# Linear attention and two MLPs on one core: the first two tiles' attention product in fp32, and w_in joined in place

## The chip, the cores and the metric

One core of a Trainium2 chip runs the whole program. The metric is the time of one execution in device microseconds. Before the change it is 1578.94 us, the median of three runs (1578.28 to 1579.91).

## The reference

```python
q_s = softmax(q, over the 64 of a head);  k_s = softmax(k, over the 576 of the sequence)
kv = einsum('bhsd,bhse->bhde', k_s, v)
x = einsum('bhsd,bhde->bhse', q_s, kv)      # 8 batches, 8 heads, 576 x 64; 1e-9 in each denominator
x = x.transpose(0, 2, 1, 3).reshape(4608, 512)
h = x @ w_in                                 # 512 x 2048
y = (maximum(h, 0) ** 2) @ w_out             # 2048 x 512
h = y @ w2_in
out = (maximum(h, 0) + alpha * minimum(h, 0)) @ w2_out
```

The weights come as float64 and are used as float32.

## The kernel before, in words

The program has four large products, one behind the other: the first MLP's hidden stage (L781, with L761 for its beginning), its projection (L1027), the second MLP's hidden stage (L1161) and its projection (L897, L902). Results between them go through DRAM. A matrix of the hidden stage and of attention is held as two fp32r parts, a head and the rest (what is left of the number when the head is taken off), and a product is three fp32r products: rest by head, head by rest, head by head (`PAIRS`). The two projections and the second hidden stage use a seven-product scheme on blocks, whose sums and differences of weights are made ahead (`Pairs.made`) during the first hidden stage and kept in DRAM (`j_dram`).

The first hidden stage goes over nine tiles of 512 tokens. For each tile `x_from_attention` makes the input x in four quarters j (two heads each): `sums` computes kv of one batch for two heads, and `rows` computes the tile's x from q and kv. `sums` loads k and v, takes the maximum of k over the sequence (a maximum over each partition's five rows, L588; a transpose on PE, L593; a maximum out of PSUM, L596; a transpose back, L599), subtracts (L603), exponentiates (L608), multiplies with v on PE in fp32 (L615), and divides: head by ACT (L625), rest by DVE (L629). `rows` does the softmax of q (L665 to L685, two of its steps on POOL), turns it on PE (L689), makes head (L692) and rest (L695), multiplies with kv in three products (L703 to L705), and makes head (L708) and rest (L711) of x. A tile of 512 tokens lies in one or two batches of 576.

w_in comes in sixteen chunks f, one for each of the tile's sixteen units of twelve products. `joined_chunk` loads a chunk of float64 (L375), lets ACT rebias the high words (L389), and DVE makes float32 of both words in two steps (L368, L369) into a second buffer `bits`; `Weights` then takes the head on ACT (L409) and the rest on POOL (L414). Two buffers (`raw`) take loads. In tile 0 the first four units run quarter by quarter (L761), so that they can start when the first quarter of x is there. ACT ends each unit with ReLU (L809) and square (L810), and SP stores it (L802).

The order on every engine is written by a planner: each step has a cost, an engine, the steps it needs, the buffers it takes and a due time, worked backwards from PE's products; `Plan.run` then lists the steps engine by engine, the earliest due first among those that can start. Instructions run in that order on their engine. `LEAD` is when the first product is due, `MADE` how far behind a place in the hidden stage a join of later weights is due. SP issues all loads and stores, in its own order.

Of the kernel before, what the change touches and what calls it, by code (L numbers as in the profile page):

```python
# [9 lines left out]
F32 = mybir.dt.float32  # L10
# [16 lines left out]
THIRD = 384  # L27
SOME = 4
# [4 lines left out]
LEAD = 28.0  # L33
APART = 9.0
TILE = 40.0
MADE = 40.0
# [10 lines left out]
def act_us(n):  # L47
    return 0.19 + n / 1200
# [202 lines left out]
def linear_attention_two_mlps(  # L251
# [61 lines left out]
    early = dict(within=(63 * KB_ // 2, 57 * KB_))  # L313
    x_early = dict(area=1, within=(64 * KB_, 154 * KB_), top=True)

    def homes(first, step, n):
# [3 lines left out]
        raw=kind(2 * BANK, 2, homes=homes(0, 4, 2)), bits=kind(BANK, 4, homes=homes(8, 2, 4)),  # L320
# [5 lines left out]
        vr0=kind(KR * 2 * D, 3, homes=homes(21, 2.5, 2) + homes(47.5, 2.5, 1)), q0=kind(2 * R * D, KB, **early),  # L326
        kvw=kind(2 * P, 2 * KB + 2, area=1, homes=homes(154, 1, 10)),
# [54 lines left out]
    def joined_chunk(kd, w, f, after, to, bits, made=None, signed=None):  # L382

        raw = buf(K["raw"])
# [6 lines left out]
        def step(n):  # L391
            join(raw.ap.bitcast(I32).rearrange("p (k f w) -> p k f w", k=2, w=2), bits().bitcast(I32))[n]()
# [3 lines left out]
        o = plan.add(lambda: step(0), "dve", 0.55, [o, made], new=[] if made else [to], use=[raw, to], lock=True)  # L396
        return o, plan.add(lambda: step(1), "dve", 0.7, [o], use=[raw, to], lock=True)

    class Weights:


        def __init__(self, kd, w):
            self.bufs, self.done = [], []
            for f in range(NF):
                bits, parts = buf(K["bits"]), buf(K["w"])
                _, o = joined_chunk(kd, w, f, None, bits, lambda bits=bits: bits.ap.rearrange("p (k n) -> p k n", k=2))
# [6 lines left out]
                def rest(bits=bits, parts=parts, e=nc.gpsimd if pool else nc.vector):  # L413
                    e.tensor_tensor(parts.ap[:, BANK:], bits.ap, parts.ap[:, :BANK].bitcast(F32), op=ALU.subtract)  # L414
# [34 lines left out]
    class Pairs:  # L449


        def __init__(self, n, kd, w, hidden, signed=None, by_product=None, turned=False):
# [4 lines left out]
            for g in range(G):  # L457
                t, f = hidden(g)
# [11 lines left out]
        def made(self, n, kd, w, g, after, due, signed):  # L470
# [11 lines left out]
            m, o0 = joined_chunk(kd, w, 2 * g, after, j, lambda: bits(0), None, signed)  # L482
            _, o1 = joined_chunk(kd, w, 2 * g + 1, after, j, lambda: bits(1), m, signed)
# [81 lines left out]
    def sums(i, j, after):  # L565
# [5 lines left out]
        km, m, rs = buf(K["km"], sbuf(2 * D)), buf(K["m"], sbuf(1)), buf(K["rs"], sbuf(1))  # L571
        ke = buf(K["ke"], sbuf(2 * KR * D))
        kvw = buf(K["kvw"], lambda g: sr[:, g * GRAIN:g * GRAIN + 2 * P].rearrange("p (n m) -> p n m", n=2))
        p1, p2, p3 = bank(K["m1"]), bank(K["m2"]), bank(K["s"])
# [47 lines left out]

        def kv_head():
# [11 lines left out]
        o = plan.add(k_max, "dve", 1.3, [lk], new=[km], use=[kt])  # L635
        lv = plan.add(lambda: load(vr, v), "sp", 2 * ISSUE, [after], new=[vr], mb=0.295)
        lv = plan.add(v_place, "act", 0.75, [lv], new=[vt], use=[vr])
        o = plan.add(k_max_t, "pe", 0.15, [o], new=[p1], use=[km])
        o = plan.add(k_max_all, "dve", 0.28, [o], new=[m], use=[p1])
# [5 lines left out]
        o = plan.add(kv_head, "act", 0.62, [o], new=[kvw], use=[p3, rs])  # L645
        o = plan.add(kv_rest, "dve", 0.56, [o], use=[p3, rs, kvw])
        kv_bufs[i, j], kv_done[i, j] = kvw, o

    def rows(i, j, after, due):

        qt, qe, qT, x = buf(K["q" if i else "q0"]), buf(K["qe"]), buf(K["qT"]), buf(K["x"])
# [70 lines left out]
        o = plan.add(q_rest, "dve", 0.7, [o], use=[pt, qT])  # L722
        o = plan.add(attend, "pe", 0.85, [o, *(kv_done[b, j] for b, *_ in parts)], new=[px], use=[qT, *kvs])
# [221 lines left out]
    def project_wide(r, stored, weights, gate):  # L945
# [3 lines left out]
        for t in range(NT // (2 * n)):  # L949
# [3 lines left out]
            def bring(b):  # L953
                k, h = divmod(b, 2)
                for q in range(G // 2):
# [8 lines left out]
                    ready[b, q] = [plan.add(load, "sp", ISSUE, after, new=[x], mb=0.393)]  # L964
# [263 lines left out]
    def x_from_attention(t):  # L1228
        gate = None
        blocks = []  # L1230
        for j in range(KB):
            if t < B:
                sums(t, j, gate)
            due = now[0] - (TILE if t > 1 else TILE1) * (1 - (j + 1) / KB) - EARLY if t else LEAD + 4 * j
# [15 lines left out]
    def signs():  # L1250
# [6 lines left out]
        0, "o", w1_out, lambda g: (1 + g // 4, 4 * (g % 4)),  # L1257
        by_product=lambda after: [(ORDER[i], "pp", "wp" if i < 4 else "wq", after[i]) for i in (4, 5, 6, 0, 1, 2, 3)],
    )
    w2i = Pairs(1, "i", w2_in, lambda g: (3 + g // 4, 4 * (g % 4)))  # L1260
    w2o = Pairs(
        2, "o", w2_out, lambda g: (5 + g // 4, 4 * (g % 4)), signed,
# [42 lines left out]
```

## Time and profile before

| | |
|---|---|
| median of three runs | 1578.94 us |
| the profiled execution | 1577.31 us |
| its span | 1575.5 us |
| PE busy | 1542.7 us (98%) |
| DVE, ACT, POOL busy | 74%, 52%, 6% |
| moved by DMA | 286.70 MB |

Busy time is from the first to the last cycle that an engine spent in instructions, without waits in between; a product's end is modelled, so that a run of products reads a little longer than its spacing. PE is the engine that is hardly ever idle. An average over the span says little of a stage: what an engine waits for in a stretch is read from that stretch.

### The profile page before, as it was taken

The page shows a single profiled execution, that of the slowest core. Times are in us where ns is not written, and L with a number is a line of the kernel's source. Part 1 is how long each engine was busy: PE and PEld are TensorE (multiplying, and loading weights), DVE is VectorE, ACT ScalarE, POOL GpSimd, SP SyncE. Part 2 cuts the span into 40 slices and gives each one's busy share as a digit, 9 for nine tenths or more (in the row PEclk, how much of TensorE's full clock was granted, in tenths as well). Part 3 has the DMA queues.
Part 4 walks back from the last instruction along what each step waited for, and adds up shares of the span by engine and source line. Part 5 has one row for each costly group of instructions (what it writes and reads, how often), then busy time and mean ns, then how long its engine had stood idle before and what let it go on. Part 6 is the DMA issues. An engine that isn't in the chain of part 4 may idle for free.

```text
span 1575.5 us, 22496 instructions
## 1 busy us (share of the span) xinstructions
PE 1542.7 (98%) x8480; PEld 1371.1 (87%) x8480; DVE 1158.7 (74%) x1671; ACT 818.1 (52%) x1244; POOL 101.4 (6%) x107
## 2 busy tenths in 40 slices
PE   4899999999999999999999999999999999999998
PEld 3678888888888999999999888888899888888887
DVE  7875666766643787777778886867778998888885
ACT  5776666767666554444445542434345344444442
POOL 4431112111100000000000000000000000000000
PEclk9999999999999999999999999999999999999999
DMA  8768878888689445325324534252466754444421
GB/s 213 213 210 274 266 247 275 276 267 284 250 286 301 136 156 186 130 89 185 138 81 167 194 148 146 111 180 97 144 209 231 233 156 134 134 134 134 134 94 34
DMA packets 196413, 286.70 MB, mean 182 GB/s; under 512 B 15568, under 2 KB 167120, under 8 KB 196304
## 3 DMA queue, kind: packets, MB, share of 16 engines
q1 hardware_dynamic: 196304, 285.27, 54.8%
q8 instruction: 66, 1.08, 0.3%
q14 instruction: 43, 0.35, 0.1%
HBM read 168.83 MB, written 116.39 MB: 181 GB/s over the span
## 4 chain that ended last, share of the span: by engine, by line
PE 94%; DMA 2%; DVE 2%; ACT 1%; issue 0%; POOL 0%; SPq 0%; DVEq 0%
PE ps L781 24%; PE ps L1161 22%; PE ps L1027 22%; PE ps L897 14%; PE ps L902 7%; PE ps L615 1%; DMA sb<-in_moe_w_in_dram 1%; PE ps L689 1%; DVE sr L548 1%; PE ps L761 1%; PE ps L704 1%; PE ps L705 1%; PE ps L703 0%; DMA sb<-j 0%; DMA sb<-in_q_dram 0%
## 5 line engine op out<-in xcount | busy, mean ns | idle before, releaser
L545 ACT CAST sr<-sb 128x768 fp32r<-128x768 f32 (+2 forms) x324 | 307.3, 972 | 291.8 <-DVE sb L842 138.1
L548 DVE TENSOR_TENSOR sr<-sb,sr 128x768 fp32r<-128x768 f32 (+2 forms) x324 | 358.3, 1124 | 107.4 <-ACT sr L545 99.2
L781 PE MATMUL ps<-sr 128*128 128x512 f32 x1680 | 405.7, 396 | 5.3 <-POOL sr L414 5.3
L781 PEld LDWEIGHTS ps<-sr 128*128 128x128 f32 x1680 | 310.6, 189 | 71.4 <-POOL sr L414 6.4
L1161 PE MATMUL ps<-sr 128*128 128x464 f32 (+1 forms) x1680 | 351.5, 371 | 0.0
L1027 PE MATMUL ps<-sr 128*128 128x384 f32 x2016 | 349.8, 334 | 0.0
L1027 PEld LDWEIGHTS ps<-sr 128*128 128x128 f32 x2016 | 349.5, 188 | 0.2
L1161 PEld LDWEIGHTS ps<-sr 128*128 128x128 f32 x1680 | 315.2, 188 | 35.3
L897 PE MATMUL ps<-sr 128*128 128x512 f32 x1008 | 275.4, 395 | 0.5 <-ACT sr L545 0.5
L1182 ACT ACTIVATE sb<-ps,sign 128x464 f32<-128x464 f32 (+1 forms) x160 | 103.2, 646 | 190.1 <-PE ps L1161 186.5
L897 PEld LDWEIGHTS ps<-sr 128*128 128x128 f32 x1008 | 172.6, 189 | 24.1 <-ACT sr L545 0.7
L902 PEld LDWEIGHTS ps<-sr 128*128 128x128 f32 x1008 | 154.6, 189 | 21.8 <-DVE sr L548 0.5
L902 PE MATMUL ps<-sr 128*128 128x256 f32 x1008 | 160.5, 281 | 0.1
L809 ACT ACTIVATE sb<-ps 128x512 f32<-128x512 f32 x144 | 85.7, 595 | 85.5 <-PE ps L781 82.6
L1188 DVE SCALAR_TENSOR_TENSOR sb<-sb,al 128x464 f32<-128x464 f32 (+1 forms) x160 | 110.6, 697 | 13.0 <-ACT sb L1182 9.3
L926 DVE TENSOR_TENSOR sb<-ps,sb 128x512 f32<-128x512 f32 x90 | 62.0, 690 | 49.9 <-ACT sb L922 27.1
L810 ACT ACTIVATE sb<-sb 128x512 f32<-128x512 f32 x144 | 91.0, 632 | 3.4
L970 DVE TENSOR_TENSOR sb<-sb 128x768 f32<-128x768 f32 x96 | 88.7, 953 | 5.4 <-DMA sb<-r 5.1
L1185 DVE SCALAR_TENSOR_TENSOR sb<-ps,sign,sb 128x464 f32<-128x464 f32 (+1 forms) x80 | 55.6, 695 | 44.8 <-PE ps L1161 39.8
L842 DVE TENSOR_TENSOR sb<-sb 128x1024 f32<-128x1024 f32 x72 | 87.8, 1220 | 0.7
L922 ACT COPY sb<-ps 128x512 f32<-128x512 f32 x36 | 21.0, 586 | 69.3 <-PE ps L902 69.3
L685 POOL TENSOR_TENSOR sb<-sb 128x512 f32<-128x512 f32 x36 | 37.8, 1052 | 246.3 <-DVE sb L681 196.0
(69 smaller groups left out, 997.9 us busy)
## 6 DMA issues: line engine op xcount, KB each, us to landing
r<-sb SPq DMA_DIRECT2D x72, 512.0 KB, 4.1
sb<-r SPq DMA_DIRECT2D x96, 384.0 KB, 4.8
sb<-r SPq DMA_DIRECT2D x72, 512.0 KB, 3.7
r<-sb SPq DMA_DIRECT2D x64, 464.0 KB, 2.7
j<-sb SPq DMA_DIRECT2D x24, 896.0 KB, 7.0
sb<-in_moe_w_in_dram SPq DMA_DIRECT2D x32, 512.0 KB, 5.2
sb<-in_moe_w_out_dram SPq DMA_DIRECT2D x32, 512.0 KB, 4.9
sb<-j SPq DMA_DIRECT2D x14, 1024.0 KB, 7.0
```

The source lines that it names most:

```text
L545: nc.scalar.copy(part(0), of(what()))
L548: nc.vector.tensor_tensor(part(1), of(what()), part(0).bitcast(F32), op=ALU.subtract)
L781: nc.tensor.matmul(h.ap, w[:, a, c, :], x_parts(x[c][0])[:, b, :], start=(c == 0 and n == 0), stop=(c == KB - 1 and n == 2),)
L810: return plan.add(lambda: nc.scalar.activation(ro.ap[:, half], ro.ap[:, half], AF.Square), "act", 0.63, [o], use=[ro])
L842: lambda x=x, y=y, z=z: nc.vector.tensor_tensor(x.ap, y.ap, z.ap, op=op), "dve", dve_us(SOME * n),
L897: nc.tensor.matmul(to, b[:, 0, g, m * P:(m + 1) * P], a, start=start and q == 0 and g == 0, stop=False, skip_group_check=True,)
L902: nc.tensor.matmul(to[:, :HALF], b[:, 1, g, m * P:(m + 1) * P], a[:, :HALF], start=False, stop=q == G // SOME - 1 and g == SOME - 1, skip_ ...
L970: lambda x=x, y=y, z=z: nc.vector.tensor_tensor(x.ap, y.ap, z.ap, op=op), "dve", dve_us(2 * n),
L1027: nc.tensor.matmul(h.ap[:, :n], a[:, u, ms], b[:, w, g], start=start and g == 0 and i == 0, stop=q == G // 2 - 1 and g == 1 and i == 2, sk ...
L1161: nc.tensor.matmul(h.ap[:, :n], a[:, u, c * P:(c + 1) * P], b[:, w], start=start and c == 0 and i == 0, stop=c == 1 and i == 2, skip_group ...
L1182: nc.scalar.mul(to, h.ap[:, :n], sign[:, by])
L1188: nc.vector.scalar_tensor_tensor(to, to, al[:, by], to, op0=ALU.mult, op1=ALU.max)
```

## The change

For the first two batches and tiles (`FIRST = 2`) kv and q stay in fp32: ACT writes kv whole (`kv_whole`) into small zeroed buffers (`kvf`, eight, zeroed by POOL at the start), the rests L629 and L695 are gone there, and attention's product is one fp32 product for each batch in the tile. In tile 2, which still reads batch 1, the batch's part is two fp32 products, with the rest and the head of q. For batch 0 (`TURNED = 1`) k is turned by PE into PSUM, in twelve fp32 products by the identity, and DVE takes the maximum of all 624 columns in one step. w_in is joined in place: the two words' result goes to the high words of the load buffer, from which ACT and POOL read every second word; `bits` is gone, and w_in has four load buffers (`raw0`). Tile 0's hidden values are stored after ReLU, and squared by ACT when the first projection has loaded them. `MADE` goes from 40 to 30; the places of the joins of later weights (`MAKE`) are the same.

```diff
+FIRST = 2
+TURNED = 1
-MADE = 40.0
+MADE = 30
...
-        raw=kind(2 * BANK, 2, homes=homes(0, 4, 2)), bits=kind(BANK, 4, homes=homes(8, 2, 4)),
+        raw=kind(2 * BANK, 2, homes=homes(0, 4, 2)), raw0=kind(2 * BANK, 4, homes=homes(0, 4, 4)),
...
+        for w in K["kvf"].homes:
+            nc.gpsimd.memset(sbuf(P)(w), 0.0)
...
         def step(n):
-            join(raw.ap.bitcast(I32).rearrange("p (k f w) -> p k f w", k=2, w=2), bits().bitcast(I32))[n]()
+            x = raw.ap.bitcast(I32).rearrange("p (k f w) -> p k f w", k=2, w=2)
+            join(x, bits().bitcast(I32) if to else x[:, :, :, 1])[n]()
...
+                def words(bits):
+                    return bits.ap.rearrange("p (f w) -> p f w", w=2)[:, :, 1]
                 def head(bits=bits, parts=parts):
-                    nc.scalar.copy(parts.ap[:, :BANK], bits.ap)
+                    nc.scalar.copy(parts.ap[:, :BANK], words(bits))
...
+        def k_turn():
+            at = 0
+            for r, n in ((0, P), (1, KF), (2, KF), (3, KF), (0, BANK - P - 3 * KF), (4, KF)):
+                for h in range(2):
+                    nc.tensor.matmul(
+                        p1.ap[h * D:(h + 1) * D, at:at + n], kt.ap[:n, h, r, :], ident[:n, :n], start=True, stop=True
+                    )
+                at += n
+        def k_max_turned():
+            nc.vector.tensor_reduce(m.ap, p1.ap[:, :BANK + KF], axis=AX.X, op=ALU.max)
...
+        def kv_whole():
+            for a, z in ((0, D), (D, 2 * D)):
+                nc.scalar.mul(kvw.ap[a:z, a:z], p3.ap[a:z, :D], rs.ap[a:z])
...
+            if i < FIRST:
+                for b, p0, p1, _ in parts:
+                    nc.tensor.matmul(
+                        o[:, :, p0:p1], kv_bufs[b, j].ap, qT.ap.rearrange("p (r t) -> p r t", r=R)[:, :, p0:p1], start=True, stop=True
+                    )
+                return
...
+                if b < FIRST:
+                    for n in (1, 0):
+                        nc.tensor.matmul(o[:, :, p0:p1], w, qs[:, n, :, p0:p1].bitcast(F32), start=n == 1, stop=n == 0)
+                    continue
...
-        o = plan.add(q_rest, "dve", 0.7, [o], use=[pt, qT])
+        if i >= FIRST:
+            o = plan.add(q_rest, "dve", 0.7, [o], use=[pt, qT])
...
+        if t * TOK < LINEAR:
+            return o
         return plan.add(lambda: nc.scalar.activation(ro.ap[:, half], ro.ap[:, half], AF.Square), "act", 0.63, [o], use=[ro])
...
+                    left = min(n, LINEAR - t0 - h * n)
+                    if left > 0:
+                        def squares(x=x, left=left):
+                            to = x.ap.rearrange("p (g t) -> p g t", g=2)[:, :, :left]
+                            nc.scalar.activation(to, to, AF.Square)
```

The planner orders everything anew. Three places show it. First PE at the start of the program, up to the first attention product (L593, L599 the transposes of k's maxima, L615 k by v, L689 the turn of q, L703 attention). Before:

```order
L593 MATMUL ps<-ident,sb 128x128 x2
L599 MATMUL ps<-ident,sb 128x128
L615 MATMUL ps<-sb 64x65 x10
L593 MATMUL ps<-ident,sb 128x128
L689 MATMUL ps<-ident,sb 128x128 x4
L599 MATMUL ps<-ident,sb 128x128 x2
L689 MATMUL ps<-ident,sb 128x128 x4
L593 MATMUL ps<-ident,sb 128x128
L615 MATMUL ps<-sb 64x65 x10
L703 MATMUL ps<-sr 128x512
```

With the change, from the second turn of k on (L613 is the turn, four rows each; L628, L644, L728, L740 are the former L599, L615, L689 and the fp32 attention product):

```order
L613 MATMUL ps<-ident,sb 64x128 x2
L613 MATMUL ps<-ident,sb 64x112 x6
L613 MATMUL ps<-ident,sb 64x48 x2
L613 MATMUL ps<-ident,sb 64x112 x2
L628 MATMUL ps<-ident,sb 128x128
L644 MATMUL ps<-sb 64x65 x10
```

A first turn of four such rows stands ahead of these; two turns are queued before the first maximum goes back (L628). The third turn follows L644, the fourth stands behind the first attention product (L740).

Second, SP from the first chunk of w_in on (L375 and L383 the chunks, L578 and L582, now L595 and L599, a load of k or v, L659, now L698, a load of q). Before:

```order
L375 DMA sb<-in_moe_w_in_dram 128x4x256
L659 DMA sb<-in_q_dram 128x2x256
L375 DMA sb<-in_moe_w_in_dram 128x4x256
L578 DMA sb<-in_v_dram 112x2x320
L582 DMA sb<-in_v_dram 16x2x64
```

With the change:

```order
L383 DMA sb<-in_moe_w_in_dram 128x4x256 x2
L698 DMA sb<-in_q_dram 128x2x256
L383 DMA sb<-in_moe_w_in_dram 128x4x256 x2
L595 DMA sb<-in_k_dram 112x2x320
L599 DMA sb<-in_k_dram 16x2x64
L595 DMA sb<-in_v_dram 112x2x320
```

Four chunks stand together, and k's fourth load behind them; before, two chunks stood ahead of it, and two loads of v and one of q that now stand behind. At the very start k's second load now stands ahead of q's first.

Third, ACT where the first projection begins (L545, now L558, heads of its operands; L809 and L810, now L859 and L862, the last ReLU and square; L1021 the new squares; L1046 and L1106 copies of results). Before:

```order
L810 ACTIVATE sb<-sb 128x512
L545 CAST sr<-sb 128x768 x5
L545 CAST sr<-sb 128x2048
L545 CAST sr<-sb 128x768
L1046 COPY sb<-ps 128x384
```

With the change:

```order
L862 ACTIVATE sb<-sb 128x512
L558 CAST sr<-sb 128x768 x2
L1021 ACTIVATE sb<-sb 128x768 x3
L558 CAST sr<-sb 128x768 x2
L1021 ACTIVATE sb<-sb 128x768
L558 CAST sr<-sb 128x768
L558 CAST sr<-sb 128x2048
L558 CAST sr<-sb 128x768
```

Eight squares of 768 elements stand behind the last unit's square, among the heads that they feed; eight of 256 elements stand earlier.

## Rows read from the trace of the kernel before

**Rows 1.** The page's first part: busy us, share of the span, instructions of each engine.
```profile
PE 1542.7 (98%) x8480; PEld 1371.1 (87%) x8480; DVE 1158.7 (74%) x1671; ACT 818.1 (52%) x1244; POOL 101.4 (6%) x107
```

**Rows 2.** Stretches: length; PE, PEld, DVE, ACT, POOL busy; granted clock, DMA share, GB/s.
```profile
0.00:32.36 32.36, 13.28 (x87) 9.16 (x87) 22.47 (x49) 15.54 (x27) 15.12 (x29) 1.00 0.77 206
32.36:50.16 17.80, 17.07 (x106) 13.18 (x104) 14.81 (x32) 11.64 (x22) 8.18 (x7) 1.00 0.69 192
50.16:106.40 56.24, 48.44 (x270) 38.23 (x269) 45.88 (x86) 44.19 (x82) 26.70 (x24) 0.97 0.75 227
```

**Rows 3.** Timeline of PE: start, us, what, idle before it.
```profile
32.36 3.01 PE L761 MATMUL ps<-sr 128*128 128x512 f32 x6
...
50.16 2.92 PE L781 MATMUL ps<-sr 128*128 128x512 f32 x12
...
66.70 5.58 PE L781 MATMUL ps<-sr 128*128 128x512 f32 x17 [2.03 <-POOL sr L414]
...
106.34 0.80 PE L615 MATMUL ps<-sb 128*64 128x65 f32 x20
```

**Rows 4.** Chain of waits, first 100 us: start, us, what.
```profile
4.09 4.74 DMA sb<-in_q_dram
...
89.47 5.34 DMA sb<-in_moe_w_in_dram
...
96.59 1.28 POOL sr L414
```

**Rows 5.** SP's waits, first 110 us.
```profile
SPq L375 <- DVE sb L369: 22.2, 10, 4.2
```

**Rows 6.** DVE's groups by shape up to 106.4 us: busy us, mean ns, idle before.
```profile
L588 DVE TENSOR_REDUCE sb<-sb 128x128 f32<-128x640 f32 x12 | 15.4, 1287 | 6.4 <-DMA sb<-in_k_dram 6.3
L603 DVE TENSOR_TENSOR sb<-sb,ps 128x640 f32<-128x640 f32 x10 | 8.1, 818 | 2.5 <-PE ps L599 1.9 <-PE ps L593 0.4
L695 DVE TENSOR_TENSOR sr<-ps,sr 128x512 fp32r<-128x512 f32 x9 | 6.1, 680 | 1.0 <-ACT sr L692 1.0
L629 DVE SCALAR_TENSOR_TENSOR sr<-ps,sb,sr 64x64 fp32r<-64x64 f32 x16 | 4.5, 279 | 0.1
L596 DVE TENSOR_REDUCE sb<-ps 128x1 f32<-128x128 f32 x11 | 3.0, 281 | 1.0 <-PE ps L593 0.9
```

**Rows 7.** Timeline of PE: fp32 products early and late, and tile 1's first attention product.
```profile
14.70 1.35 PE L615 MATMUL ps<-sb 128*64 128x65 f32 x20 [4.95 <-ACT sb L608]
...
27.01 0.47 PE L599 MATMUL ps<-ident,sb 128*128 128x128 f32 x1
27.61 1.12 PE L689 MATMUL ps<-ident,sb 128*128 128x128 f32 x4
...
49.02 0.60 PE L689 MATMUL ps<-ident,sb 128*128 128x128 f32 x4
...
52.92 0.27 PE L593 MATMUL ps<-ident,sb 128*128 128x128 f32 x1
52.94 0.28 PE L703 MATMUL ps<-sr 128*128 128x64 f32 x1
53.05 0.28 PE L704 MATMUL ps<-sr 128*128 128x64 f32 x1
...
53.97 0.27 PE L599 MATMUL ps<-ident,sb 128*128 128x128 f32 x1
```

**Rows 8.** Timeline of DVE: the last step of tile 0's first and fourth quarter.
```profile
32.05 0.69 DVE L711 TENSOR_TENSOR sr<-ps,sr 128x512 fp32r<-128x512 f32 x1
...
43.31 0.69 DVE L711 TENSOR_TENSOR sr<-ps,sr 128x512 fp32r<-128x512 f32 x1 [0.54 <-ACT sr L708]
```

**Rows 9.** ACT's groups up to 106.4 us: the squares.
```profile
L810 ACT ACTIVATE sb<-sb 128x512 f32<-128x512 f32 x16 | 10.1, 629 | 0.2
```

**Rows 10.** A stretch in which the first projection begins, columns as in rows 2.
```profile
520.00:540.00 20.00, 20.00 (x117) 20.00 (x116) 17.82 (x21) 11.56 (x15) 0.00 (x0) 1.00 0.39 122
```

**Rows 11.** Timeline of PE: the first projection's beginning.
```profile
518.66 11.63 PE L1027 MATMUL ps<-sr 128*128 128x384 f32 x66
```

More of the change, by code (lines that the diff above doesn't have):

```diff
@@ L27 @@
 THIRD = 384
+LINEAR = 512
 SOME = 4
@@ L32 @@
 MM2 = 0.12
-LEAD = 28.0
+FIRST = 2
+TURNED = 1
+LEAD = 28
+STEP = 4
 APART = 9.0
 TILE = 40.0
-MADE = 40.0
+MADE = 30
+MAKE = (1, 7)
 EARLY = 6.0
@@ L309, in bank @@
         return Buf(kd, lambda ns: ps[:, ns[0] * BANK:(ns[-1] + 1) * BANK])
-    early = dict(within=(63 * KB_ // 2, 57 * KB_))
+    early = dict(within=(63 * KB_ // 2 + 2 * KB_ * FIRST, 57 * KB_))
     x_early = dict(area=1, within=(64 * KB_, 154 * KB_), top=True)
@@ L391, in step @@
         def step(n):
-            join(raw.ap.bitcast(I32).rearrange("p (k f w) -> p k f w", k=2, w=2), bits().bitcast(I32))[n]()
+            x = raw.ap.bitcast(I32).rearrange("p (k f w) -> p k f w", k=2, w=2)
+            join(x, bits().bitcast(I32) if to else x[:, :, :, 1])[n]()
         o = plan.add(lambda: load_chunk(kd, w, f, raw), "sp", ISSUE, [after], new=[raw], mb=0.524)
         o = plan.add(rebias, "act", 0.67, [o, signed], use=[raw])
-        o = plan.add(lambda: step(0), "dve", 0.55, [o, made], new=[] if made else [to], use=[raw, to], lock=True)
-        return o, plan.add(lambda: step(1), "dve", 0.7, [o], use=[raw, to], lock=True)
+        o = plan.add(lambda: step(0), "dve", 0.55, [o, made], new=[] if made or not to else [to], use=held, lock=True)
+        return o, plan.add(lambda: step(1), "dve", 0.7, [o], use=held, lock=True), raw
     class Weights:
@@ L634, in sums @@
         lk = plan.add(lambda: load(kt, k), "sp", 2 * ISSUE, [after], new=[kt], mb=0.295)
-        o = plan.add(k_max, "dve", 1.3, [lk], new=[km], use=[kt])
+        if not turned:
+            o = plan.add(k_max, "dve", 1.3, [lk], new=[km], use=[kt])
         lv = plan.add(lambda: load(vr, v), "sp", 2 * ISSUE, [after], new=[vr], mb=0.295)
         lv = plan.add(v_place, "act", 0.75, [lv], new=[vt], use=[vr])
-        o = plan.add(k_max_t, "pe", 0.15, [o], new=[p1], use=[km])
-        o = plan.add(k_max_all, "dve", 0.28, [o], new=[m], use=[p1])
+        if turned:
+            o = plan.add(k_turn, "pe", 2.1, [lk], new=[p1], use=[kt])
+            o = plan.add(k_max_turned, "dve", 0.82, [o], new=[m], use=[p1])
+        else:
+            o = plan.add(k_max_t, "pe", 0.15, [o], new=[p1], use=[km])
+            o = plan.add(k_max_all, "dve", 0.28, [o], new=[m], use=[p1])
         o = plan.add(k_max_back, "pe", 0.1, [o], new=[p2], use=[m])
@@ L644, in sums @@
         o = plan.add(kv_sum, "dve", 0.4, [o], new=[rs], use=[p3])
-        o = plan.add(kv_head, "act", 0.62, [o], new=[kvw], use=[p3, rs])
-        o = plan.add(kv_rest, "dve", 0.56, [o], use=[p3, rs, kvw])
+        o = plan.add(kv_whole if whole else kv_head, "act", 0.62, [o], new=[kvw], use=[p3, rs])
+        if not whole:
+            o = plan.add(kv_rest, "dve", 0.56, [o], use=[p3, rs, kvw])
         kv_bufs[i, j], kv_done[i, j] = kvw, o
     def rows(i, j, after, due):
-        qt, qe, qT, x = buf(K["q" if i else "q0"]), buf(K["qe"]), buf(K["qT"]), buf(K["x"])
+        qt, qe, qT, x = buf(K["q" if i else "q0"]), buf(K["qe"]), buf(K["qf" if i < FIRST else "qT"]), buf(K["x"])
         mx, sm = buf(K["mx"], sbuf(2 * R)), buf(K["sm"], sbuf(2 * R))
@@ L721, in rows @@
         o = plan.add(q_head, "act", 0.6, [o], new=[qT], use=[pt])
-        o = plan.add(q_rest, "dve", 0.7, [o], use=[pt, qT])
-        o = plan.add(attend, "pe", 0.85, [o, *(kv_done[b, j] for b, *_ in parts)], new=[px], use=[qT, *kvs])
+        if i >= FIRST:
+            o = plan.add(q_rest, "dve", 0.7, [o], use=[pt, qT])
+        o = plan.add(attend, "pe", 0.85 if i > FIRST else 1.1, [o, *(kv_done[b, j] for b, *_ in parts)], new=[px], use=[qT, *kvs])
         o = plan.add(x_head, "act", 0.6, [o], new=[x], use=[px])
@@ L963, in bring @@
                     raw[b, q] = x
-                    ready[b, q] = [plan.add(load, "sp", ISSUE, after, new=[x], mb=0.393)]
+                    o = plan.add(load, "sp", ISSUE, after, new=[x], mb=0.393)
+                    left = min(n, LINEAR - t0 - h * n)
[3 more added lines that the diff above has]
+                            nc.scalar.activation(to, to, AF.Square)
+                        o = plan.add(squares, "act", act_us(2 * left), [o], use=[x])
+                    ready[b, q] = [o]
             def combine(to, one, two, op):
@@ L1233, in x_from_attention @@
                 sums(t, j, gate)
-            due = now[0] - (TILE if t > 1 else TILE1) * (1 - (j + 1) / KB) - EARLY if t else LEAD + 4 * j
+            due = now[0] - (TILE if t > 1 else TILE1) * (1 - (j + 1) / KB) - EARLY if t else LEAD + STEP * j
             blocks.append(rows(t, j, gate, due))
```

34 lines of the change are left out of this document (20 added, 14 removed).

## The prediction

> **What bounds the kernel now.** I read the share of busy time first, then the stretches of the first 106 us, then the timeline of PE, the chain of waits and SP's waits, and last the single durations. PE is busy for 98% of the span [rows 1], so 32.8 us of the 1575.5 are idle, and the stretches say where: 19.1 us before 32.36, 0.7 us from there to 50.16, and 7.8 us from 50.16 to 106.40 [rows 2]. These sum to 27.6; behind 106 PE runs practically without a break up to the last stage. So only what moves the first 106 us can move the end.
>
> Three times in them matter [rows 3]. At 32.36 the first product of the first projection starts, on a quarter of tile 0's attention output; at 50.16 the first unit that uses all four quarters; at 106.34 tile 0's sixteenth unit is done, and tile 1 follows without a wait. The longest single wait of the last stretch, 2.03 us, ends on POOL's L414, the last step of a chunk of w_in [rows 3]. The chain behind such a chunk is to be seen in [rows 4]: a load of 5.34 us, rebias on ACT, two joins on DVE, the head on ACT, the rest on POOL until 97.87. SP's loads wait 22.2 us, ten times, for the second join of an earlier chunk [rows 5]: there are two buffers for loads, and DVE gives them back. DVE is busy 45.88 of the 56.24 us and ACT 44.19 [rows 2]. So the first 106 us are bound by DVE and ACT work and by two load buffers, and PE pays with waits. That wait of 2.03 us, after others, is followed by 17 products in 5.58 us, 0.33 us each, where twelve at 50.16 took 0.24 each [rows 3]; the granted clock over the stretch is 0.97 [rows 2]. PE had sat idle for those 2.03 us just before.
>
> **The change, part by part**, against the profiled execution's 1577.31 us (span 1575.5).
>
> *DVE work.* For batch 0 the maximum over 640 strided elements (L588, 1.287) and the one out of PSUM (L596, 0.281) become one read of 624 elements of PSUM. No row shows it. Below it is bounded by L603, which reads PSUM for 640 elements in 0.818; above by L588's 1.287. I take 0.82, the row that reads the same memory at the same length: 4 x (1.287 + 0.281 - 0.82) = 3.0 us less. The rest of q goes in tiles 0 and 1: 8 x 0.680 = 5.4 us. The rest of kv goes: 16 x 0.279 = 4.5 us. Together 12.9 of DVE's 83 us [rows 6]. By the order of the instructions, counted with the mean durations of their groups, DVE has 76.2 us of work up to the second join of the sixteenth chunk before and 60.9 after; the 2.4 us beyond 12.9 are the third tile's work that now stands behind it.
>
> *ACT work.* Tile 0's sixteen squares (0.629 each, 10.1 us [rows 9]) go. Thirteen of them stood ahead of the sixteenth chunk's head: 8.2 us less.
>
> *Load buffers.* Joining in place, w_in has four buffers to load into in place of two, but each is now kept until POOL has read it (L414, 1.3 us at the end [rows 4]). Four loads now go out before the fourth k. The joins' strides are not new to DVE's reads; the strided writes and reads on ACT and POOL are. ACT's rebias already runs on every second word. I put the strides at nothing, since four buffers cover some tenths of a us in a chunk's chain. Without that cover, and were POOL slower by half, 0.65 us would come on top for each of sixteen chunks, 10 us in all, against the 29.5 us that POOL idles in the third stretch [rows 2].
>
> *PE work.* Turning k takes 12 fp32 products of 64 columns of weights, and fp32 products are two instructions each in the trace (10 products of L615 are x20). A turn streams 2 x 624 columns, twice: 2496. L615, which also fills the halves of the partitions in turn, takes 1.35 us for 20 x 65 columns early on, 1.04 ns a column: 2.6 us a turn. L689, whole width, takes 1.12 us for 4 with a single one at 0.477 [rows 7]; (1.12 - 0.48)/3/128 = 1.67 ns: 4.2 us a turn. I take 2.6, since the shape is that of L615, and keep 4.2 for the range. The first two turns run before the first shift, beside loads that PE waits for anyway (it is idle 19 of the first 32 us). The attention product in fp32 is 2 x 512 columns: at L689's later rate, (0.60 - 0.27)/3/128 = 0.86 ns [rows 7], 0.88 us against three of 0.24 = 0.73. In tile 0 that adds 0.15 x 4 = 0.6. In tile 1 it takes 0.88 in place of 1.03 (52.94 to 53.97 [rows 7]): 0.6 less. In tile 2 batch 1's 128 columns take 4 x 128 x 0.86 = 0.44 in place of three of 0.11: 0.4 more. I book 0.6 us more in all, between none and 1.5.
>
> *The sum.* (a) The start. The fourth quarter's last instruction on DVE started at 43.31, the first quarter's at 32.05 [rows 8]. Up to the first, DVE now has 3.7 us less to do, up to the fourth 4.9 us less. Against this stands that DVE's first step now waits for q, issued behind two more loads and 4.74 us on its way [rows 4], so not before 8.3. I take 3.7 us: the full units begin at 46.5. Its ends are 2 us later (turns of 4.2, below) and 6 earlier. (b) The idling. PE's content from 50.16 to 106.40 is 48.44, less 1.7 for the low clock: 46.7. Without a wait sixteen units end at 93.2, and the last chunk is needed at 90.3. DVE, 82% busy, gains 15.3/0.82 = 19 us on its 98; ACT, 79% busy, gains 8.2/0.79 = 10, so the chunk comes at about 88. It fits, with little to spare; I leave 2.5 of the 7.8 us: 5.3 gained, between 0 and 7.8. (c) With short waits the clock doesn't fall: 1.6, between 0 and 1.7. (d) PE's extra: -0.6.
>
> 3.7 + 5.3 + 1.6 - 0.6 = 10.0 us less: 1567.3 for the profiled execution. That lies 1.6 below the median of the runs, so **1569** in terms of the median. The ends of the four terms together reach from 3.5 slower to 15.5 faster.
>
> *The squares' new place.* They come back, 10 us of ACT, at the start of the first projection, where ACT is busy for 11.56 of 20 us and DVE for 17.82 [rows 10]. The third of the seven products is the first that needs squares of full width (768 elements, 768/512 x 0.629 = 0.94). It starts 96 products after the stage does: 96 x 0.176 = 16.9 us (66 in 11.63 [rows 11]). ACT has six conversions, four squares and one conversion of 2048 between the last unit and it, about 11 us. So I put it at nothing; cover gone, eight squares of 0.94 are 7.5 us.
>
> The table of joins for the later weights gets due 10 us earlier; DVE is far less busy there, and PE had no wait: nothing.
>
> **The rivals.**
> 1. *The turns of k are slow.* If the halves don't run beside each other, a turn is 4.2 us by L689. Two of them stand ahead of the first shift in PE's queue and the fourth ahead of the last one. The first quarter then comes about 2 us later than now: (a) is -1 to -2, 5.3 + 1.6 - 0.6 - 1.4 = 4.9 less: 1574.0. Against it L615's 1.04 ns. [...] Chance 0.2.
> 2. *The loads are the bound, and it gets slower.* By 100 us the DMA engines are 0.69 to 0.77 busy [rows 2]. Two more chunks ahead of the fourth k are 1.05 MB, at the 227 GB/s of the third stretch 4.6 us. If k comes that much later, DVE, which runs in order, stands at batch 0's last maximum; (a) is -3.7, the chunks are no faster, (d) stays: 4.3 slower, 1583.2. It decides if k now lands behind those chunks by more than DVE's 3.7 us. Against it: q and v loads that stood ahead of this k now stand behind it. Chance 0.07.
> 3. *The squares stall the first projection.* 7.5 us of squares less the 16.9 - 11 that I count as cover, wrong by enough to show some 5 us: 1574. For it speaks DVE, 0.89 busy there. Chance 0.1.
> 4. *It doesn't speed the chunks.* ACT in order, or DVE stalls in new places, leave the 7.8 us of waits and the low clock: only 3.7 - 0.6 = 3.1 are left, 1575.8. Chance 0.1.
>
> The forecast has 0.53.
>
> **How the numbers follow.** 0.2%, 3.2 us, is about what a measurement of this kernel can tell. The forecast and the first rival are faster by more, the third mostly, half of the fourth not: faster 0.80. Same takes the rest of rivals 3 and 4 and a weak first rival: 0.12. Slower: rival 2 and a tail, 0.08. The range leaves out rival 2 and the far ends: 1562.5 to 1576.5.
>
> **What would show it.** Right: the first product of the first projection before 31 us, the first full unit at 45 to 48, tile 0's last unit before 98, less than 3.5 us of PE idling in between, SP's waits for a join of w_in much shorter; the first projection starts without a wait. A turn of k lasts 2.6 us. Wrong: a turn of 4 us, k's fourth load landing after 26, PE still waiting more than 5 us for the rest of the chunks (L427 in the changed kernel), or a wait at the first products of the first projection.

## The result, and the profile after

The changed kernel takes 1562.67 us, the median of four runs (1561.85 to 1563.34), beside 1578.61 for the kernel before in the same session (1576.63 to 1579.91): a ratio of 0.9900, 95% interval 0.9883 to 0.9917. The forecast was 1569, its range 1562.5 to 1576.5; the result stands at the range's lower end. The profiled execution is 1562.07 us, its span 1560.3, against 1577.31 and 1575.5: 15.2 us of span.

The page's first part, to be held against [rows 1]:

```profile
PE 1543.4 (99%) x8564; PEld 1371.7 (88%) x8564; DVE 1148.2 (74%) x1643; ACT 818.1 (52%) x1244; POOL 104.0 (7%) x115
```

PE's busy time is 0.7 us more than before and its idle time 16.9 us in place of 32.8. So the gain is idle time of PE, and it comes from the first 115 us. Two stretches show it, first of the kernel before, from the first full unit to the 288th product of w_in (48 run by quarters, 240 in full units: tile 1's eighth unit) and the rest behind it. Columns as in rows 2.

```profile
50.16:129.70 79.54, 71.74 (x411) 57.40 (x411) 56.97 (x114) 57.44 (x107) 29.55 (x26) 0.98 0.75 229
129.70:1575.50 1445.80, 1440.60 (x7882) 1291.32 (x7882) 1064.44 (x1477) 733.44 (x1090) 48.56 (x47) 1.00 0.53 179
```

The same of the changed kernel, the start ahead of them; these answer to [rows 2]:

```profile
0.00:29.77 29.77, 18.23 (x178) 12.65 (x178) 20.89 (x43) 16.35 (x28) 16.41 (x37) 0.96 0.91 246
29.77:45.64 15.87, 15.87 (x101) 11.94 (x102) 13.19 (x25) 12.96 (x26) 10.00 (x9) 0.98 0.75 214
45.64:115.30 69.66, 69.49 (x407) 55.48 (x407) 50.96 (x100) 49.34 (x90) 28.73 (x24) 1.00 0.84 259
115.30:1560.30 1445.00, 1439.81 (x7884) 1291.60 (x7884) 1063.20 (x1478) 739.45 (x1102) 48.84 (x47) 1.00 0.53 179
```

I read the 15.2 us in three parts. The first full unit starts at 45.64 in place of 50.16: 4.5. From there to product 288 it takes 69.66 in place of 79.54: 9.9, of which 7.6 are idle time (7.80 to 0.17) and 2.3 PE's busy time. Of these, some 1.5 are the low clock: behind the wait at 66.70, 24 products took 7.17 us, where 24 take 5.72 at 85.60 in the changed kernel. The granted clock was 0.83 from 60 to 70 us in the kernel before, and it is 1.00 over the changed kernel's middle. Behind product 288 the gain is 0.8. These three columns (**start**, **middle**, **rest**) are the measure for every experiment below. PE's timeline of the kernel before, for this stretch:

```profile
66.70 7.17 PE L781 MATMUL ps<-sr 128*128 128x512 f32 x24 [2.03 <-POOL sr L414]
...
90.59 5.72 PE L781 MATMUL ps<-sr 128*128 128x512 f32 x24 [2.08 <-POOL sr L414]
...
97.92 8.49 PE L781 MATMUL ps<-sr 128*128 128x512 f32 x36 [0.95 <-POOL sr L414]
```

Two readings of the prediction are wrong by these lines. Its longest single wait, 2.03, has one of 2.08 behind it. And 106.34 is not the end of tile 0's sixteenth unit, but of the unit after it, tile 1's first: from 50.16 to there PE does 156 products in full units, and tile 0 has 144. Tile 0 ended at about 103.6, with the first 24 of the 36 products that start at 97.92; in the changed kernel it ends at 88.5.

PE's timeline, to be held against [rows 3, 7]; start, us, what, idle before it:

```profile
4.95 5.26 PE L613 MATMUL ps<-ident,sb 128*64 128x128 f32 x48 [4.95 <-DMA sb<-in_k_dram]
...
14.16 2.71 PE L613 MATMUL ps<-ident,sb 128*64 128x128 f32 x24
16.81 0.33 PE L628 MATMUL ps<-ident,sb 128*128 128x128 f32 x1
16.98 0.60 PE L728 MATMUL ps<-ident,sb 128*128 128x128 f32 x4
...
19.49 0.80 PE L644 MATMUL ps<-sb 128*64 128x65 f32 x20 [0.94 <-ACT sb L637]
...
22.08 1.61 PE L613 MATMUL ps<-ident,sb 128*64 128x128 f32 x24 [0.73 <-DMA sb<-in_k_dram]
...
29.77 1.77 PE L811 MATMUL ps<-sr 128*128 128x512 f32 x5 [0.41 <-DVE sr L760]
...
45.64 3.02 PE L831 MATMUL ps<-sr 128*128 128x512 f32 x12
...
62.35 3.01 PE L831 MATMUL ps<-sr 128*128 128x512 f32 x12 [0.17 <-ACT sb L859]
...
85.60 5.72 PE L831 MATMUL ps<-sr 128*128 128x512 f32 x24
```

The two first turns of k take 2.63 us each, the third 2.71, the fourth 1.61. One single product of L811 stands at 27.94 already; the work is continuous from 29.77, and the 0.17 at 62.35 is the only wait between there and product 288. Of PE's waits for the rest of a chunk (L414 in [rows 3]) none is left; a load of weights still waits once for one, 0.2 us. The sixteenth chunk's rest is done at 85.20, by POOL's line below, and PE starts the sixteenth unit at 85.60.

```profile
83.89 1.31 POOL L427 TENSOR_TENSOR sr<-sb,sr 128x512 fp32r<-128x512 f32 x1 [0.44 <-ACT sr L422]
```

SP's waits for a chunk's buffer ([rows 5]: 22.2 us, ten) are now these:

```profile
SPq L383 <- POOL sr L427: 13.1, 8, 3.2
```

The buffer comes back later in a chunk's life than before, from POOL and not from DVE, and SP waits less all the same.

DVE's groups in the first 100 us (columns as in rows 6):

```profile
L619 DVE TENSOR_REDUCE sb<-ps 128x1 f32<-128x624 f32 x4 | 3.1, 782 | 1.3 <-PE ps L613 1.3
L376 DVE TENSOR_SCALAR sb<-sb 128x512 int32<-128x512 int32 x18 | 9.0, 498 | 0.1
L377 DVE SCALAR_TENSOR_TENSOR sb<-sb 128x512 int32<-128x512 int32 x18 | 16.8, 934 | 0.3
```

A maximum out of PSUM takes 0.782. Of L376, the first step of a join, the last column matters: DVE idles 0.1 us ahead of all 18, while the kernel before idled 3.0 us there (L368).

### The profile page after: what moved, and what is told of

Read it like the earlier page. It is cut to its first block, busy times and chain, and to the rows that moved or that the text cites. A ratio compares the mean times of both kernels' runs of the same rounds, so it can differ in the third digit from the quotient of the medians.

```text
span 1560.3 us, 22647 instructions
## 1 busy us (share of the span) xinstructions
PE 1543.4 (99%) x8564; PEld 1371.7 (88%) x8564; DVE 1148.2 (74%) x1643; ACT 818.1 (52%) x1244; POOL 104.0 (7%) x115
## 4 chain that ended last, share of the span: by engine, by line
PE 97%; DMA 2%; DVE 1%; issue 0%; ACT 0%; SPq 0%
PE ps L831 24%; PE ps L1221 22%; PE ps L1087 22%; PE ps L949 15%; PE ps L954 8%; PE ps L644 1%; PE ps L728 1%; PE ps L811 1%; DMA sb<-in_moe_w_out_dram 0%; PE ps L753 0%; PE ps L754 0%; DMA sb<-in_moe_w_in_dram 0%; PE ps L752 0%; PE ps L740 0%; DMA sb<-in_q_dram 0%; DMA sb<-in_k_dram 0%
## 5 line engine op out<-in xcount | busy, mean ns | idle before, releaser
L558 ACT CAST sr<-sb 128x768 fp32r<-128x768 f32 (+2 forms) x324 | 307.4, 971 | 286.2 <-DVE sb L894 139.9
L859 ACT ACTIVATE sb<-ps 128x512 f32<-128x512 f32 x144 | 85.7, 595 | 59.4 <-PE ps L831 53.3
L978 DVE TENSOR_TENSOR sb<-ps,sb 128x512 f32<-128x512 f32 x90 | 61.9, 690 | 50.2 <-ACT sb L974 26.1
L862 ACT ACTIVATE sb<-sb 128x512 f32<-128x512 f32 x128 | 80.9, 632 | 3.5
```

The costliest lines, as they stand in the source:

```text
L558: nc.scalar.copy(part(0), of(what()))
```

## The experiments

Twelve kernels, each profiled and timed beside the kernel before. Medians in us; start, middle and rest as above, from each kernel's own trace.

| kernel | median | ratio to before, interval | start | middle | rest |
|---|---|---|---|---|---|
| before | 1578.61 | | 50.2 | 79.5 | 1445.8 |
| changed | 1562.67 | 0.9900 (0.9883 to 0.9917) | 45.6 | 69.7 | 1445.0 |
| join alone | 1577.23 | 0.9992 (0.9983 to 1.0001) | 52.6 | 79.0 | 1443.6 |
| fp32 part alone | 1572.27 | 0.9957 (0.9943 to 0.9971) | 47.1 | 75.4 | 1447.3 |
| all but the join | 1570.50 | 0.9942 (0.9925 to 0.9959) | 48.3 | 78.0 | 1443.3 |
| all but the squares | 1567.98 | 0.9928 (0.9913 to 0.9942) | 48.0 | 72.5 | 1445.1 |
| all but fp32 and turns | 1572.05 | 0.9959 (0.9944 to 0.9974) | 51.5 | 73.2 | 1444.7 |
| all but the turns | 1576.29 | 0.9980 (0.9971 to 0.9990) | 54.5 | 68.1 | 1453.6 |
| turns, without fp32 | 1572.51 | 0.9959 (0.9944 to 0.9974) | 51.2 | 74.9 | 1444.9 |
| two load buffers | 1582.05 | 1.0020 (1.0010 to 1.0029) | 48.7 | 82.5 | 1448.9 |
| later joins due at 40 | 1566.79 | 0.9920 (0.9906 to 0.9933) | 46.6 | 69.7 | 1447.4 |
| changed, due 31 | 1564.93 | 0.9907 (0.9890 to 0.9923) | 46.5 | 71.4 | 1445.9 |
| before, due 31 | 1579.96 | 0.9999 (0.9988 to 1.0010) | 51.7 | 83.2 | 1443.3 |
| fourth buffer for k | 1572.84 | 0.9959 (0.9946 to 0.9971) | 50.4 | 68.3 | 1450.6 |

The kernel before was timed again beside each group of runs, with medians from 1578.6 to 1579.4, so differences of medians between rows are good to about 1 us. The start has a scatter of its own: in the changed kernel, with the due time 31, with the later joins due at 40 and without the move of the squares, all engines run the same instructions in the same order up to about 43 us, and yet the first full unit comes at 45.64, 46.54, 46.55 and 47.96.

Counts of DVE's work in the expectations are a bit low, since they left some 0.5 us of each of softmax's sums (L718) out. Counted again with the mean durations of the changed kernel's trace (the second step of a join at its usual 0.69), DVE has up to the sixteenth chunk's second join 81.0 us before, 65.5 in the changed kernel, 81.7 with the join alone, 79.7 without fp32 and turns, 76.7 with turns alone, 75.4 without the join, 70.0 with fp32 alone, 67.5 without the squares' move.

### Is it only another order?

Both kernels were planned anew with one due time moved.

```diff
-LEAD = 28
+LEAD = 31
```

> The changed kernel with only the due time of tile 0's first product moved from 28 to 31: the same instructions in another order. Order theory (a re-planned order is worth several us by itself, so that the parts' losses in the first four runs are mostly the luck of the order): 3 us or more away from the changed kernel's 1562.7, either way. Work and buffer theories: DVE's work up to the sixteenth chunk is the same within 0.1 us (57.5 against 57.6), so within 2 us of it, 1561 to 1564.7.

> The kernel before with the due time of tile 0's first product moved from 28 to 31, as the run on the changed kernel had it: same instructions, another order. If the gain is in the work and the buffers, another order of the old work can't reach it: 1576 to 1583, 7 us or more of PE idling between 30 and 110 us. If the old order was an unlucky one: 1571 or less.

The changed kernel becomes 2.3 us slower (1.5 when each is set against its own timing of the kernel before), the old one 0.6 us in its own comparison, within its interval. So these two shifts of the order are worth a us or two in all, and the old order was no unlucky one by this test; the middle alone moves by 1.7 and 3.7 us (71.4 and 83.2). They don't bound what an order can cost: in two runs below the rest is 5.6 and 8.6 us longer by waits far behind the edit. Parts are therefore valued by the three columns and not by medians alone, and differences under about 4 us between experiments are not read as the worth of a part.

### The join in place

Alone, in the kernel before but for it (the squares' place, fp32, the turns and the due time of later joins undone):

```diff
-FIRST = 2
-TURNED = 1
-LINEAR = 512
-MADE = 30
+FIRST = 0
+TURNED = 0
+LINEAR = 0
+MADE = 40
```

> Only the join in place with four load buffers is kept; kv, q, the maxima and the squares are as before. Work theory (the gain is DVE and ACT work taken off the first 100 us): by the order DVE has 73.6 us of work up to the sixteenth chunk's second join, 76.2 before, 57.6 in the changed kernel, so hardly anything is gained: first product of the first projection at 32 us, 5 us or more of PE idling between it and tile 0's end, 1574 to 1578. Buffer theory (the gain is that loads no longer wait for a join): first product at 32 us too, but the idling goes from 8.5 to under 2 us, SP's waits for a join of w_in fall under 14 us, 1565 to 1569.

The work theory's figure, and the buffer theory is out as it stood: the buffers alone bring nothing. SP waits as long as before, 22.4 us, now for POOL, and PE still waits for chunks and, longer, for a maximum of k. Waits of SP's queue, then of PE, first 110 and 130 us:

```profile
SPq L383 <- POOL sr L427: 22.4, 8, 7.9
```

```profile
PE ps L831 <- POOL sr L427: 3.6, 3, 1.7
PE ps L628 <- DVE sb L625: 3.5, 1, 3.5
```

Then the reverse: everything but the join in place.

```diff
-raw0=kind(2 * BANK, 4, homes=homes(0, 4, 4))
+bits=kind(BANK, 4, homes=homes(8, 2, 4))
...
-        raw = buf(K["raw"]) if to else buf(K["raw0"])
+        raw = buf(K["raw"])
...
-                _, o, bits = joined_chunk(kd, w, f, None, None, None)
+                bits = buf(K["bits"])
+                _, o, _ = joined_chunk(kd, w, f, None, bits, lambda bits=bits: bits.ap.rearrange("p (k n) -> p k n", k=2))
...
-                    return bits.ap.rearrange("p (f w) -> p f w", w=2)[:, :, 1]
+                    return bits.ap
```

> Everything of the change but the join in place: w_in has two load buffers and four for the joined words again. Work theory: first product before 30.5 us, under 2 us of PE idling behind it, 1562 to 1566. Buffer theory: first product before 30.5 us, but 5 us or more of PE idling behind it, SP's waits for a join about 20 us, 1568 to 1573.

Here the buffer theory's figure comes out: 7.8 us of the changed kernel's gain are gone, in the middle (78.0 against 69.7). Two load buffers make DVE wait ahead of a join, for ACT's rebias of a chunk that came late; the group on DVE, idle in its last column:

```profile
L376 DVE TENSOR_SCALAR sb<-sb 128x512 int32<-128x512 int32 x16 | 8.6, 538 | 5.0 <-ACT sb L398 5.0
```

What PE then waits for is not the chunk but what stands behind that wait on DVE and ACT, attention of later tiles (L663, L655, L606 are L662, L654, L605 with line numbers one higher). Waits of PE from 40 to 130 us:

```profile
PE ps L753 <- DVE sr L663: 3.6, 1, 3.6
PE ps L741 <- ACT sb L655: 1.3, 1, 1.3
PE ps L623 <- DVE sb L606: 1.0, 1, 1.0
```

SP's waits for a join are a miss of that theory: 9.8 us in five, where it named about 20; SP waits as long, 11.1 us, to load k (for the shift on DVE, L633). So how much of the 7.8 is the buffers' alone and how much the order's is not split.

Third, in place with two buffers only:

```diff
-raw0=kind(2 * BANK, 4, homes=homes(0, 4, 4))
+raw0=kind(2 * BANK, 2, homes=homes(0, 4, 2))
```

> The whole change, but with two load buffers for w_in in place of four, joined in place. Buffer theory: a buffer is kept from the load to the rest on POOL (load about 5, rebias 0.7, joins 1.5, head 0.7, rest 1.3, 9 us or more), so two of them bring a chunk each 4.6 us at best and sixteen take 74 us from the first load at 9, 83 or later with any wait: 5 us or more of PE idling, 1569 to 1578. If the number of buffers hardly matters once DVE and ACT have less to do: under 2 us of idling, 1562 to 1565.

19.4 us slower than the changed kernel and slower than the kernel before by 0.1 to 0.3%, beyond the bracket given. The middle is 82.5, with 4.1 us of idling in later tiles on top. So joining in place has a price by this run, a buffer held from load to POOL; it pays because it makes room for four.

### The fp32 part and the turns of k

```diff
-FIRST = 2
-TURNED = 1
+FIRST = 0
+TURNED = 0
```

> The join in place and the new place of the squares stay; kv, q and k's maxima are as before. Work theory: DVE has 71.7 us of work up to the sixteenth chunk's second join against 57.6, first product at 32 us or later, 3 us or more of PE idling behind it, 1571 to 1576. Buffer theory: first product at 32 us, idling under 1.5 us, 1564 to 1568.

1572.05, the work theory's figure; the first product comes at 32.06 and the full units at 51.5, later than in the kernel before. The start is the fp32 part's. Its two halves apart, first without the turns (`TURNED = 0`), then with them and without fp32 (`FIRST = 0`):

> k's maxima of batch 0 are taken on DVE again as before, the rest of the change stays. Work theory: up to tile 0's first quarter DVE has 20.0 us of work against 15.9, up to the sixteenth chunk 59.8 against 57.6; the first product comes 1 to 3 us later, little idling behind it: 1564 to 1567. If the turns cost as much on PE's path as they save on DVE: 1561.5 to 1564, first product before 30.5.

> kv and q are split in two parts again in tiles 0 and 1, with attention in three products; the turns of k, the join in place and the squares' place stay. Work theory: DVE has 67.8 us up to the sixteenth chunk against 57.6: 2 to 6 us of PE idling behind the first product, 1567 to 1571. If the fp32 part is worth little and the turns carry the gain: 1562 to 1565.

Without the turns it is 13.6 us slower, far outside both expectations. The start is the latest of all, 54.5: the fp32 rests are gone, but batch 0's maxima still go over DVE, in order, and PE idles 22.9 of the first 54.5 us. The middle is as good as the changed kernel's, or better (68.1). The rest is 8.6 us longer, though nothing in it differs by design. PE's timeline shows where:

```profile
362.77 0.29 PE L628 MATMUL ps<-ident,sb 128*128 128x128 f32 x1 [1.21 <-DVE sb L625]
...
366.29 0.33 PE L752 MATMUL ps<-sr 128*128 128x128 f32 x1 [1.25 <-DVE sr L662]
...
369.07 1.35 PE L644 MATMUL ps<-sb 128*64 128x65 f32 x20 [2.23 <-ACT sb L637]
370.35 4.94 PE L831 MATMUL ps<-sr 128*128 128x512 f32 x11
```

The planner put a late tile's attention where its chain has no cover; 4.7 us of waits, and then 11 products in 4.94 us, 0.45 each, at a granted clock of 0.50 from 370 to 375, where the 27 from 354.73 on took 0.23 each. By span it is 8.8 us more in the start, 1.5 less in the middle and 8.6 more in the rest. The start's are the turns'. The rest's are put down to the new order: the same three waits appear in the run with a fourth buffer for k (below), which has the turns. The run with turns and without fp32 has a start of 51.2. Each half alone leaves the start behind the old 50.2; only both give 45.6.

The fp32 part with its turns alone (old join, squares behind each ReLU, `MADE = 40`):

> Only the fp32 part (kv, q and k's turns) is kept: two load buffers and four for joined words again, squares behind each ReLU, the later joins due as before. Additive theory (each part has its own gain; leaving the fp32 part out of the changed kernel cost 9.4 us): about 1570. Chain theory (the parts share one path and each uncovers the next; the fp32 part and the squares together gained 8.3, the squares on top of the join 5.2): 3 to 4 us gained, 1574.5 to 1577, with the full units starting before 49 but 5 us or more of PE idling behind them.

6.8 us, between the two figures: neither additive nor a mere chain. Its start is 47.1, 1.4 us later than the changed kernel's; its middle is 75.4, with 4.0 us of idling, and SP waits for a join of w_in as before:

```profile
SPq L383 <- DVE sb L377: 20.8, 9, 3.9
```

### The squares

```diff
-LINEAR = 512
+LINEAR = 0
```

> Tile 0's squares stand again behind each ReLU. Work theory with ACT as part of the bound (8 us of squares ahead of the sixteenth chunk's head): 2 to 4 us of PE idling come back before tile 0's end, 1564.5 to 1567. If ACT has slack in tile 0 now that chunks come early: no change, 1562 to 1563.5, idling under 0.5 us.

5.3 us slower, a little beyond the work theory's figure. But only the middle (72.5 against 69.7) can be the squares': up to about 43 us all engines have the same instructions in the same order in both kernels, and yet this one is 2.3 us behind by then (the third turn of q in tile 0 starts at 36.17, in the changed kernel at 33.85), a lag that stays the same up to the first full unit. It is 0.9 by 13 us: DVE's first step waits for q until 8.56, in the changed kernel until 7.88. It is 1.1 when the continuous work starts (30.91 against 29.77), and the rest comes from PE's own durations behind that. The kernel with squares behind each ReLU:

```profile
17.99 1.06 PE L728 MATMUL ps<-ident,sb 128*128 128x128 f32 x4
...
20.98 1.35 PE L644 MATMUL ps<-sb 128*64 128x65 f32 x20 [0.87 <-ACT sb L637]
...
30.91 1.50 PE L811 MATMUL ps<-sr 128*128 128x512 f32 x5 [1.84 <-DVE sr L760]
32.34 1.35 PE L644 MATMUL ps<-sb 128*64 128x65 f32 x20
33.63 1.65 PE L811 MATMUL ps<-sr 128*128 128x512 f32 x3
```

The last two steps take 0.80 and 0.96 in the changed kernel (at 31.46 and 32.19). The granted clock from 30 to 40 us is 0.83 here and 0.97 there; ahead of it PE had waited 1.84 us for DVE here, 0.41 there. The first two steps, too, take 0.60 and 0.80 in the changed kernel (at 16.98 and 19.49), but that lag, 2.7 us at its largest, is mostly gone by 30.91, since PE then waits for DVE in both. So about 3 of the 5.3 us stand in the middle, where PE idles 2.1 us, 1.0 of it for chunks; 2.3 stand where the kernels don't differ. And 3 us is no more than a new order did to the middle (1.7 and 3.7 with the due time 31): the squares' worth is likely and small, and not measured apart. Of this kernel's four runs one took 1564.83; it has no profile, so that its start came earlier is not shown.

The prediction put the squares' return at nothing. PE in the changed kernel, at the start of the first projection:

```profile
469.77 32.35 PE L831 MATMUL ps<-sr 128*128 128x512 f32 x142
501.96 18.21 PE L1087 MATMUL ps<-sr 128*128 128x384 f32 x104
```

There is no wait.

### The due time of later joins

```diff
-MADE = 30
+MADE = 40
```

> The changed kernel with the joins of later weights due as late as before (40 in place of 30). The instructions up to the sixteenth chunk stand in the same order on DVE. Prediction's reading (PE had no wait there, it is worth nothing): 1561.5 to 1564. If the later joins then come too late or run into attention's work of tiles 2 to 7: 1565 or more, with PE waits behind 110 us.

The middle is the same, as it should be. The start is 0.9 us later, with the same order up to there, so by scatter; 2.4 us are lost behind the middle, 1.23 of them in one wait at 166.97. The prediction's "nothing" doesn't hold in this order, by an amount near that of any new order.

### An attempt at a faster start

```diff
-k0=kind(KR * 2 * D, 3, homes=homes(16, 2.5, 2) + homes(45, 2.5, 1))
+k0=kind(KR * 2 * D, 4, homes=homes(16, 2.5, 2) + homes(45, 2.5, 1) + homes(50, 2.5, 1))
```

> The changed kernel with a fourth load buffer for k (the fourth load waits for the first shift on DVE otherwise, and lands behind four chunks at 22 us). By the order k's fourth load now stands ahead of all chunks and its turn ahead of the first attention product. If the start is bound by that load: the turn ends before 20, the first product of the first projection comes 1 to 3 us earlier, 1559.5 to 1561.5. If DVE or the loads of the chunks (DMA engines 0.9 to 1.1 busy to 24 us) bound the start: the first product no earlier, 1562 to 1565.

The fourth turn does end earlier, at 19.1 in place of 23.7, and the kernel is 10.2 us slower than the changed one. Start 50.4: PE now waits 2.74 and 3.00 us for the exponentials of k (L637); on DVE the second shift (L632, 21.33) waits 1.10 us for ACT, and the third and fourth (26.39) stand behind five steps of joins and a sum. And the same three waits as in the run without turns (1.21, 1.25, 2.24) appear at 358 to 365. The fourth load of k was not what set the start. Nothing tried beats the changed kernel.

## Why the prediction was right, and what in it was mis-sized

It forecast 10.0 us less and got 15.2 in the profiled execution (15.9 in the medians), by the mechanism it named. Step by step:

- **The start (a).** Forecast 3.7 earlier, measured 4.5: full units at 45.64, in the 45 to 48 named. The three runs with the same order up to there have 46.54, 46.55 and 47.96, so the profiled execution was an early one, and the forecast's 46.5 lies among them. The argument counted DVE's work. The halves show that this count is not enough: without the turns DVE has about as much to do up to tile 0's last quarter as before (33.2 against 34.1, counted the same way) and the start is 4.3 us later. What decides is the chain from k to the first quarter, in order on DVE: in that run 10.9 of the 22.9 us that PE idles end with k's maximum there (L605).
- **The idling (b), the clock (c), the extra work (d).** Together 6.3 forecast, 9.9 measured in the middle. This is the mis-sized term. (b) left 2.5 of 7.8 us idle, on the ground that the last chunk comes at about 88 and PE needs it at 90.3; 0.17 is left. Both times were off. 90.3 rests on 106.34 as tile 0's end; without tile 1's first unit it would have been about 87.5, ahead of the chunk. But the chunk came 3 us earlier than forecast: POOL's last L427 ends at 85.20, and PE starts the sixteenth unit at 85.60. The two errors went against each other, and that the forecast still had the chunk in time is luck. (c) 1.6 was forecast; the 24 products above show 1.5. That short waits keep the clock up was the author's estimate, and no run shows it as a rule: the granted clock is 1.00 over the changed kernel's middle, with 0.17 us of waits, but in the kernel before it is 1.00 from 86 to 96 us as well, across the wait of 2.08. (d) was booked as 0.6 more. PE's busy time in the middle fell by 2.25, so it was some 0.8 less there: tile 1's fp32 attention product takes 0.63 us from its start at 48.61 to the next one's, where its three products took 1.03 so counted, and a few instructions (407 for 411) have moved behind the middle.
- **A turn of k.** Forecast 2.6, measured 2.63, 2.63 and 2.71, and 1.61 for the fourth, at 22.08, where other fp32 products were shorter too (L644 0.80 at 19.49, 1.35 at 13.03). Rival 1 is out: its 4.2, an estimate from L689's row, is above each of the four turns. The sum in the prediction stood on L615's row.
- **The maximum out of PSUM.** Taken at 0.82 from L603, measured 0.782, a little below the bound that L603's 0.818 was taken for.
- **The strides.** At nothing on POOL: L427's mean is 1.33 us, L414's was 1.35, so reading every second word shows no cost there (medians 1.314 and 1.290). On ACT the strided head costs 0.661 against 0.613, 0.8 us over sixteen, which no wait of PE shows.
- **Four buffers "cover some tenths of a us".** Understated. This was the one part whose removal shows 8 us in the middle. The prediction treated the buffers as a cover for strides and gave the idling's gain to DVE's and ACT's lighter work. The runs show that both are needed: buffers alone leave the middle at 79.0, lighter work without them at 75.4 to 78.0, join and squares at 73.2, join and fp32 at 72.5, all at 69.7. The last two steps, 3.5 and 2.8, are within what an order alone did.
- **The squares.** 8.2 us of ACT were counted as coming off the chunks' chain; the run without that move has a middle 2.8 us longer, of which the part that isn't order is open. No stall at the first projection: rival 3 is out.
- **Rival 2** (loads bind, slower) had k's fourth load land behind the chunks; it landed at 22.08, PE waited 0.73 us for it, and the run that brought it forward was slower. **Rival 4** is out by the 0.17 us.

## What to carry to other kernels

One late buffer held up what stood on DVE behind the instruction that waited for it: in the run without the join in place, DVE's 5.0 us of waiting for a chunk came out at PE as waits for attention (3.6, 1.3 and 1.0 us). Four buffers paid only together with taking work off the same engine: they alone leave the middle at 79.0 against 79.5, and with the rest of the change they bring it from 78.0 to 69.7. So value parts of such a change together, and run each both alone and left out. Where a planner writes the order, split the span at a few fixed products before reading a difference: half of a part's apparent worth can stand 300 us later, where the new order put waits (without the turns, 8.6 of 15.9 us of span).

## What the runs showed that was not expected

- The turns are not only cheaper than they look, in the profiled execution they are followed by faster products. In the kernel before, the turn of q takes 1.12 us at 27.61 [rows 7]; in the changed kernel the same four products take 0.60 at 16.98. PE did some 8 us of turns between 4.95 and 16.87 there and was busy for 9.52 of these 11.92 us, in the kernel before for 3.30. It isn't so each time: behind the same turns they take 1.06 at 17.99 without the squares' move, and 1.06 at 17.47 with later joins due at 40.
- The granted clock on the page reads 1.00 up to 24 us in both kernels, while equal products differ by a factor of 1.7 (L644 1.35 at 13.03, 0.80 at 19.49). What makes the difference is not shown. With later joins due at 40 the column reads 0.89 over the first 30 us, and L644 takes 1.35 at 13.42 there as well, 0.80 at 20.46.
- The second step of a join on DVE has a longer mean in the changed kernel. The group in the kernel before, then in the run with everything but the join in place:

```profile
L369 DVE SCALAR_TENSOR_TENSOR sb<-sb 128x512 int32<-128x512 int32 x16 | 12.5, 784 | 0.3
```

```profile
L377 DVE SCALAR_TENSOR_TENSOR sb<-sb 128x512 int32<-128x512 int32 x16 | 11.3, 704 | 0.2
```

In the changed kernel the mean is 934 (above): twelve of its 18 take 0.64 to 0.69 as in the others, six 0.93 to 1.77. The place of the result is not the reason, since the kernel before has two such steps (1.42 and 1.54). The traces show what they have in common. The slowest one on DVE, and POOL at the same time:

```profile
68.60 1.77 DVE L377 SCALAR_TENSOR_TENSOR sb<-sb 128x512 int32<-128x512 int32 x1
```

```profile
68.51 1.31 POOL L427 TENSOR_TENSOR sr<-sb,sr 128x512 fp32r<-128x512 f32 x1 [1.94 <-ACT sr L422]
```

DVE's step starts 0.09 us into POOL's instruction and ends 0.55 after it. In the first 130 us of the fourteen traces 49 of these steps take over 0.75 us; every one started while a TENSOR_TENSOR of POOL ran, and ended 0.55 to 0.56 us after that. Of the eight faster ones that started so, seven found POOL with under 0.2 us to go. So in these traces the end of a slow step follows the end of POOL's instruction. The six cost 4.5 us of DVE, the two in the kernel before 1.6; that is more than the strides on ACT and POOL that the prediction weighed.
